# A written order for TensorE and VectorE in the first stage of a three-stage kernel, from its second tile on

## The chip, the cores and the metric

The kernel runs on one core of a Trainium2 chip. The metric is the device time of one execution in microseconds (us). A core has TensorE (PE, matmuls and transposes), VectorE (DVE), ScalarE (ACT), GpSimd (POOL) and SyncE (SP, which issues the transfers here). Each has an instruction queue of its own and waits on semaphores for the others. Matmuls write PSUM, eight banks; everything else lives in SBUF or in DRAM.

## What is computed

Three computations follow one another. Attention runs in chunks of 64 tokens, for 8 heads of 64; its output, 4608 tokens by 512, goes through an RMS norm and a gated layer of width 1536, and the result through a second layer of width 2048:

```python
attn = softmax(scale * q @ k.T) @ v                  # per chunk of 64 tokens and head
x = attn / rms(attn) * rms_g                         # [4608, 512]
x = (silu(x @ w_gate) * (x @ w_val)) @ moe_w_out     # 512 -> 1536 -> 512
h = x @ w_in                                         # 512 -> 2048
out = (h * cos(h)) @ moe2_w_out                      # 2048 -> 512
```

The weights arrive as 64-bit words and are converted on the chip to pairs of 32-bit numbers (a high and a low part). Every product of two such pairs is three matmuls (high by high, high by low, low by high).

## The kernel before, in words

The kernel is one Python function that traces instructions; a scheduler then puts them in an order for each engine and adds the semaphores. The scheduler works with a model of the engines and may move an instruction ahead of one that was written earlier, as long as no dependency forbids it. Tiles come from pools: a tag with `bufs=n` has n buffers, and who takes a buffer again waits until its last readers are done.

The first stage does attention, the norm and the gated product. It goes over 9 tiles of 512 tokens. The first tile is done in halves of 256 tokens, while the gate and value weights are still being converted. The changed loop covers the other eight tiles, `i` from 1 to 8.

In a tile, `gated(f, ...)` runs for 12 blocks of columns `f`: 12 matmuls into a PSUM tile `g`, then 12 into `v`; ScalarE computes `sg` = Silu of `g`, and VectorE multiplies it with `v` into `h`, which is stored to DRAM (`hd`) in pairs of `f`. `g` and `v` have three PSUM buffers each. The operand is `xt`, the normed attention output of the tile, as a high and a low part.

Between these groups stand other pieces of work, placed by `Slots`: a counter that goes up after the `g` and again at the end of every `gated`, so 24 slots in a tile. `slots.after(k, fn)` runs `fn` in k slots from now. Two kinds of work are placed so:

- Attention for the next tile, two pairs of 128-token units in a tile. A pair has six steps (`ATT`). `att_s`: scores `sc` on TensorE, then on VectorE the row maximum `mx` and the difference `p`. `att_e`: Exp on ScalarE. `att_n`: VectorE divides by the row sum `z`. `att_t`: TensorE transposes `p` into `pt`, ScalarE copies it to `pts`. `att_v`: TensorE makes `o`; ScalarE squares it and sums (the instruction writes `xn` and `ss`), GpSimd makes the factor `rs`, VectorE the normed `xn`. `att_x`: TensorE transposes `xn` into `tr`; ScalarE casts it to the high part of `xt`, VectorE subtracts for the low part. `sc`, `pt`, `o` and `tr` share two PSUM buffers.
- Weight conversions for the later stages, 44 in all (`w_tick`). One takes a raw block that was loaded earlier (two buffers), turns it into `wt` (Abs on ScalarE, L102, then four instructions on VectorE, L103 to L106), splits it with a cast on ScalarE and a subtraction on VectorE (L109, L110), and stores `wout` to DRAM (`kout` or `kin`). Of the 44, 28 are of a long kind (for the two output weights), which makes four sums `wsum` besides (L185) and has two casts and two subtractions; 16 are of a short kind. `wt`, `wsum` and `wout` have one buffer each: the casts of a conversion wait until the store of the one before has landed.

Stages two (`b<-xo,w` with 384 columns), three (`h<-xt,w`) and four (`b<-w,xo`) follow and are not touched.

Of the kernel before, what the change touches and what calls it, by code (L numbers as in the profile page):

```python
# [25 lines left out]
N1 = F1 // P  # L26
# [6 lines left out]
TILE = 512  # L33
# [14 lines left out]

HI_MIN = 2.0**-15
HI_MAX = (1.875 - 2.0**-14) * 2.0**16  # L50

AHEAD = 5

# [15 lines left out]
def kernel(  # L69
# [25 lines left out]
    def f32(a):  # L95
        return a.bitcast(F32)


    def convert(raw, t):
        w = raw.bitcast(U32).rearrange("p (n t) -> p n t", t=2)  # L100
        lo, hi = w[:, :, 0], w[:, :, 1]
        nc.scalar.activation(f32(t), f32(hi), AF.Abs)  # L102
        nc.vector.tensor_scalar(f32(t), f32(t), HI_MIN, HI_MAX, op0=ALU.max, op1=ALU.min)  # L103
        nc.vector.tensor_scalar(t, t, 3, 0x3FFFFFF8, op0=ALU.logical_shift_left, op1=ALU.bitwise_and)
        nc.vector.scalar_tensor_tensor(t, hi, 0xC0000000, t, op0=ALU.bitwise_and, op1=ALU.bitwise_or)
        nc.vector.scalar_tensor_tensor(t, lo, 29, t, op0=ALU.logical_shift_right, op1=ALU.bitwise_or)  # L106

    def split(to, a, eng):
        nc.scalar.copy(to[:, 0], a)  # L109
        eng.tensor_tensor(to[:, 1], a, f32(to[:, 0]), op=ALU.subtract)  # L110
# [12 lines left out]
    def free(*tags):  # L123
        for tag in tags:
            if not wanted:
                return
            key = kind, i, k = wanted.pop(0)
            place_of[key] = tag
            if kind in ("h", "x2", "g"):
                early[key] = wp.tile([P, 2, H if kind == "h" else D], F32, tag=tag, name="a")  # L130
                rows = slice(0, 2) if kind == "h" else slice(2 * k, 2 * k + 2)
                a = {"h": hd[0][:, k], "x2": x2d[0], "g": gd[0][:, 0]}[kind]
                nc.sync.dma_start(out=early[key], in_=a[:, rows, : early[key].shape[-1]])
                continue
            shape = [P, 2, D] if kind == "in" else [P, 2, 2, 2, P]
            weight[key] = wp.tile(shape, F32R, tag=tag, name="w")
            nc.sync.dma_start(out=f32(weight[key]), in_=kept[kind, i] if kind == "in" else kept[kind, i][:, k])
# [6 lines left out]
    raws = []  # L144
    flip = [0]

    def w_load():
        if todo_w and len(raws) < 2:
            kind, i, half = todo_w.pop(0)
            flip[0] ^= 1  # L150
            raw = wp.tile([P, 4, P], U64, tag=f"p{24 + flip[0]}", name="wraw")
            if kind == "in":
                nc.sync.dma_start(out=raw, in_=w2[i, 0].rearrange("p (a b) -> p a b", b=P))
            else:

                a, m = (w1, 2) if kind == "out1" else (w2, 1)
                c = 4 * (i // 2) + i % 2
                for n, (row, b) in enumerate(((c, 0), (c + 2, 0), (c + 2, 1), (c, 1))):
                    o = b * 2 * P + half * P
                    nc.sync.dma_start(out=raw[:, n, :], in_=a[row, m][:, o : o + P])  # L160
            raws.append((kind, i, half, raw))

    def w_tick():
        if not raws:
            return
        kind, i, half, raw = raws.pop(0)
        t = pp.tile([P, 4, P], U32, tag="pt", name="wt")
        convert(raw.rearrange("p a b -> p (a b)"), t.rearrange("p a b -> p (a b)"))
        t = f32(t)
        if kind == "in":  # L170
            to = pp.tile([P, 2, D], F32R, tag="pout", name="wout")
            split(to, t.rearrange("p a b -> p (a b)"), nc.vector)
            kept[kind, i] = dr.tile([P, 2, D], F32, name=f"kin{i}")
            nc.sync.dma_start(out=kept[kind, i], in_=f32(to))
        else:
            s = pp.tile([P, 4, P], F32, tag="ps", name="wsum")

            if kind == "out1":
                ops = ((t[:, 3, :], t[:, 2, :], ALU.add), (s[:, 0, :], t[:, 0, :], ALU.subtract))
                ops += ((t[:, 0, :], t[:, 3, :], ALU.subtract), (t[:, 1, :], s[:, 1, :], ALU.subtract))  # L180
            else:
                ops = ((t[:, 3, :], t[:, 0, :], ALU.subtract), (t[:, 2, :], s[:, 0, :], ALU.subtract))
                ops += ((t[:, 2, :], t[:, 3, :], ALU.subtract), (t[:, 1, :], s[:, 1, :], ALU.subtract))
            for n, (a, b, op) in enumerate(ops):
                nc.vector.tensor_tensor(s[:, n, :], a, b, op=op)  # L185
            to = pp.tile([P, 2, 7, P], F32R, tag="pout", name="wout")
            split(to[:, :, 0:3, :], t[:, :3, :], nc.vector)
            split(to[:, :, 3:7, :], s, nc.vector)
            g, e = i // 2, i % 2
            if (kind, g) not in kept:  # L190
                kept[kind, g] = dr.tile([P, 7, 2, 2, 2, P], F32, name=f"k{kind}{g}")
            for h in range(2):
                nc.sync.dma_start(out=kept[kind, g][:, :, e, h, half], in_=f32(to[:, h]))
        w_load()
# [49 lines left out]
    def mm3(acc, steps, first):  # L244

        n = len(steps)
        for k, (ah, al, bh, bl) in enumerate(steps):
            for q, (a, b) in enumerate(((ah, bh), (ah, bl), (al, bh))):
                nc.tensor.matmul(  # L249
                    acc, a, b, start=first and k == 0 and q == 0, stop=k == n - 1 and q == 2, skip_group_check=True  # L250
                )
# [21 lines left out]
    with ExitStack() as st:  # L273
# [117 lines left out]
        xts = {}  # L391
# [16 lines left out]
        ATT = (att_s, att_e, att_n, att_t, att_v, att_x)  # L408
        slots = Slots()
# [19 lines left out]
        def gated(f, x, t0, n):  # L429

            acc = []
            for m in range(2):
                z = ps_g.tile([P, D], F32, tag="gv"[m], name="gv"[m])[:, :n]
                ww = w[f, m]
                c = [slice(d * P, (d + 1) * P) for d in range(ND)]
                mm3(z, [(ww[:, 0, c[d]], ww[:, 1, c[d]], x[:, 0, d], x[:, 1, d]) for d in range(ND)], True)
                acc.append(z)
                if m == 0:
                    slots.end()
            sg = tp.tile([P, D], F32, tag="sg", name="sg", bufs=2)[:, :n]  # L440
            nc.scalar.activation(sg, acc[0], AF.Silu)  # L441
            if f % 2 == 0:
                pend[t0] = tp.tile([P, 2, D], F32, tag="h", name="h")[:, :, :n]
            h = pend[t0]
            nc.vector.tensor_tensor(h[:, f % 2], sg, acc[1], op=ALU.mult)  # L445
            if f % 2:
                c = t0 % PIECE
                nc.sync.dma_start(out=hd[t0 // PIECE][:, f // 4, f % 4 - 1 : f % 4 + 1, c : c + n], in_=h)
            slots.end()
# [27 lines left out]
        for k in range(N1 + BEHIND):  # L477
            need1(min(k + 1, N1 - 1))
            for b in range(2):
                f = k - BEHIND * b  # L480
                if 0 <= f < N1:
                    gated(f, xts[0][:, :, :, b * half : (b + 1) * half], b * half, half)
        ntile = NT // TILE
        for i in range(1, ntile):
            if i + 1 < ntile:
                for u in (4 * i + 4, 4 * i + 6):
                    for n, f in enumerate(ATT):
                        slots.after(1 + 11 * ((u % 4) // 2) + 2 * n - n // 3, lambda f=f, u=u: f(u))
            for n in range(6):
                slots.after(2 + 4 * n, w_tick)  # L490
            for f in range(N1):
                gated(f, xts[i], i * TILE, TILE)
                if i == ntile - 1:
                    if f == 0:
                        while raws:
                            w_tick()
                        free("p24", "p25", "p26", "p27")
                    free(f"p{2 * f}", f"p{2 * f + 1}")
        slots.flush()


# [74 lines left out]
    with ExitStack() as st:  # L576
# [3 lines left out]
        raw, xts = {}, {}  # L580
        ntile = NT // TILE
# [56 lines left out]
    with ExitStack() as st:  # L638
# [53 lines left out]
        def add(a, b, tag="o", bufs=3):  # L692
            t = block(tag, bufs)
            nc.vector.tensor_tensor(t, a, b, op=ALU.add)
            return t
# [8 lines left out]
        u = add(z[6], s1, "s6", 1)  # L704
# [79 lines left out]
```

## Time and profile before

| | |
|---|---|
| median of 3 runs | 1796.24 us (1793.16 to 1796.95) |
| the profiled execution | 1800.6 us |
| span in its profile, first to last instruction | 1798.8 us |
| mean granted TensorE clock | 0.985 of full |
| TensorE busy, of the span | 1727.4 us (96%) |
| VectorE busy | 1232.4 us (69%) |
| ScalarE busy | 756.6 us (42%) |

A row of the profile names the line, the engine, the operation, and what it writes and reads; `x12` is a count of instructions that were merged into the row. In brackets stands how long the engine was idle before it, and what ended that. Line numbers are those of the kernel before; in the changed kernel the same lines stand two lower, and from line 484 on three.

### The profile page before, as it was taken

What the parts mean: (1) busy time and instruction counts of PE and PEld (TensorE: products, weight loads), DVE (VectorE), ACT (ScalarE), POOL (GpSimd) and SP (SyncE); (2) the same over time, 40 slices, a digit from 0 to 9 for tenths busy, and PEclk for the clock granted to TensorE, in tenths of its full rate; (3) what the DMA queues carried; (4) which work ended last, traced back from release to release, by engine and by line L of the source; (5) the groups of instructions that cost most, each with busy time, mean ns of one, the idle gap of its engine ahead of it and who ended that gap; (6) DMA issues with size and microseconds to landing.
All of it is one profiled execution on the core that took longest, in us unless ns stands there. A gap on an engine that the chain in (4) does not pass through costs nothing.

```text
span 1798.8 us, 29151 instructions
## 1 busy us (share of the span) xinstructions
PE 1727.4 (96%) x11736; PEld 1539.2 (86%) x11736; DVE 1232.4 (69%) x1825; ACT 756.6 (42%) x1117; POOL 49.3 (3%) x92
## 2 busy tenths in 40 slices
PE   5899899999999999899999999999999899999998
PEld 5897787778888888799999888888888799999998
DVE  6888787787333331477777588888887887777775
ACT  5544455454333321244444344444443444444443
POOL 1210000000000000000000000000000000000000
PEclk8999999999999999999999999999999899999999
DMA  9338877888222216643335743333225823344430
GB/s 368 112 118 265 260 267 255 252 257 255 83 94 82 83 48 221 211 176 141 141 141 204 264 164 123 124 118 123 100 94 186 304 95 118 123 145 142 147 119 30
DMA packets 159799, 294.72 MB, mean 164 GB/s; under 512 B 10288, under 2 KB 96304, under 8 KB 155184
## 3 DMA queue, kind: packets, MB, share of 16 engines
q1 hardware_dynamic: 159664, 292.86, 47.8%
q8 instruction: 92, 1.51, 0.4%
q14 instruction: 43, 0.35, 0.1%
HBM read 173.80 MB, written 119.01 MB: 163 GB/s over the span
## 4 chain that ended last, share of the span: by engine, by line
PE 78%; issue 9%; DVE 5%; DMA 3%; ACT 3%; POOL 2%; SPq 0%; ACTq 0%; DVEq 0%; POOLq 0%
PE b L249 34%; PE h L249 22%; PE v L249 10%; PE g L249 10%; DMA kout<-wout 3%; POOL w L110 1%; PE sc L315 1%; PE pt L354 1%; PE tr L402 1%; DVE wout L110 1%; PE o L368 0%; POOL rs L387 0%; ACT wout L109 0%; DVE h L445 0%; ACT wt L102 0%
## 5 line engine op out<-in xcount | busy, mean ns | idle before, releaser
L249 PE MATMUL h<-xt,w 128*128 128x512 f32 x1728 | 392.3, 389 | 1.3 <-ACT xt L109 1.2
L249 PEld LDWEIGHTS h<-xt,w 128*128 128x128 f32 x1728 | 324.2, 188 | 69.2 <-ACT xt L109 1.5
L249 PE MATMUL b<-w,xo 128*128 128x256 f32 x3024 | 369.9, 285 | 11.7 <-ACT s L723 5.4
L249 PEld LDWEIGHTS b<-w,xo 128*128 128x128 f32 x3024 | 367.3, 194 | 14.5 <-ACT s L723 7.0
L249 PE MATMUL v<-xt,w 128*128 128x512 f32 (+1 forms) x1440 | 327.3, 376 | 2.5 <-POOL w L110 1.6
L249 PE MATMUL g<-xt,w 128*128 128x512 f32 (+1 forms) x1440 | 325.0, 375 | 4.3 <-ACT w L109 2.1
L249 PEld LDWEIGHTS g<-xt,w 128*128 128x128 f32 x1440 | 254.6, 192 | 50.4 <-ACT w L109 2.3
L249 PEld LDWEIGHTS v<-xt,w 128*128 128x128 f32 x1440 | 255.7, 192 | 48.7 <-POOL w L110 2.4
L249 PE MATMUL b<-xo,w 128*128 128x384 f32 x1512 | 266.5, 335 | 12.4 <-ACT s L559 5.7
L249 PEld LDWEIGHTS b<-xo,w 128*128 128x128 f32 x1512 | 261.7, 188 | 17.4 <-ACT s L559 7.6
L241 DVE TENSOR_TENSOR xo<-rawg,xo 128x512 fp32r<-128x512 f32 x210 | 142.6, 688 | 80.1 <-ACT xo L240 78.8
L240 ACT CAST xo<-rawg 128x512 fp32r<-128x512 f32 x210 | 128.3, 620 | 159.3 <-PE b L249 96.3
L445 DVE TENSOR_TENSOR h<-sg,v 128x512 f32<-128x512 f32 (+1 forms) x120 | 75.3, 629 | 173.8 <-PE v L249 172.1
L441 ACT ACTIVATE sg<-g 128x512 f32<-128x512 f32 (+1 forms) x120 | 66.2, 552 | 171.7 <-PE g L249 155.3
L625 ACT ACTIVATE k<-h 128x1024 int32<-128x1024 f32 x72 | 73.5, 1021 | 142.2 <-PE h L249 142.2
L241 DVE TENSOR_TENSOR xo<-rawh,xo 128x768 fp32r<-128x768 f32 x102 | 94.1, 954 | 51.6 <-ACT xo L240 51.6
L612 ACT ACTIVATE r<-r,halfpi 128x1024 f32<-128x1024 f32 x72 | 82.5, 1145 | 91.2 <-DVE r L611 91.2
L240 ACT CAST xo<-rawh 128x768 fp32r<-128x768 f32 x102 | 81.8, 835 | 89.0 <-DMA rawh<-hd 41.4
L609 DVE SCALAR_TENSOR_TENSOR r<-k,h 128x1024 f32<-128x1024 int32 x72 | 87.6, 1217 | 39.9 <-ACT k L625 39.9
L613 DVE TENSOR_TENSOR r<-r,h 128x1024 f32<-128x1024 f32 x72 | 87.6, 1216 | 34.2 <-ACT r L612 34.1
L610 DVE SCALAR_TENSOR_TENSOR r<-k,r 128x1024 f32<-128x1024 int32 x72 | 87.8, 1220 | 0.9
L109 ACT CAST wout<-wt 128x384 fp32r<-128x384 f32 (+1 forms) x44 | 24.3, 552 | 123.4 <-DMA kout<-wout 63.9
(85 smaller groups left out, 1281.0 us busy)
## 6 DMA issues: line engine op xcount, KB each, us to landing
gd<-r SPq DMA_DIRECT2D x72, 512.0 KB, 2.6
rawg<-gd SPq DMA_DIRECT2D x35, 1024.0 KB, 7.3
kout<-wout SPq DMA_DIRECT2D x56, 448.0 KB, 4.4
w<-kout SPq DMA_DIRECT2D x49, 512.0 KB, 4.2
hd<-h SPq DMA_DIRECT2D x48, 512.0 KB, 3.6
rawh<-hd SPq DMA_DIRECT2D x15, 1536.0 KB, 8.7
qk<-in_qk_dram SPq DMA_DIRECT2D x36, 512.0 KB, 5.2
wraw<-in_w_dram SPq DMA_DIRECT2D x112, 128.0 KB, 3.5
```

The costliest lines, as they stand in the source:

```text
L109: nc.scalar.copy(to[:, 0], a)
L110: eng.tensor_tensor(to[:, 1], a, f32(to[:, 0]), op=ALU.subtract)
L240: nc.scalar.copy(o[:, 0], a)
L241: nc.vector.tensor_tensor(o[:, 1], a, f32(o[:, 0]), op=ALU.subtract)
L249: nc.tensor.matmul(acc, a, b, start=first and k == 0 and q == 0, stop=k == n - 1 and q == 2, skip_group_check=True)
L441: nc.scalar.activation(sg, acc[0], AF.Silu)
L445: nc.vector.tensor_tensor(h[:, f % 2], sg, acc[1], op=ALU.mult)
L609: nc.vector.scalar_tensor_tensor(r, k, -PI2_HI, h, op0=ALU.mult, op1=ALU.add)
L610: nc.vector.scalar_tensor_tensor(r, k, -PI2_LO, r, op0=ALU.mult, op1=ALU.add)
L612: nc.scalar.activation(r, r, AF.Sin, bias=halfpi)
L613: nc.vector.tensor_tensor(r, r, h, op=ALU.mult)
L625: nc.scalar.activation(k, h, AF.Copy, scale=INV2PI, bias=0.25)
```

## The change

The loop over the eight tiles is put into `tc.manual_schedule(engines=ORDERED)` with TensorE and VectorE: on these two engines the scheduler keeps the order in which the instructions are written. ScalarE, GpSimd and SyncE are ordered by the scheduler as before. The slots of the attention steps change too: before, a tile's first pair stood at slots 1, 3, 5, 6, 8, 10 and its second at 12, 14, 16, 17, 19, 21; now at 0, 1, 3, 6, 8, 10 and 12, 13, 15, 18, 20, 22. The conversions keep their slots (2, 6, 10, 14, 18, 22), but are no longer moved from there on VectorE.

```diff
+ET = mybir.EngineType
+ORDERED = {ET.PE, ET.DVE}
...
         ntile = NT // TILE
-        for i in range(1, ntile):
-            if i + 1 < ntile:
-                for u in (4 * i + 4, 4 * i + 6):
-                    for n, f in enumerate(ATT):
-                        slots.after(1 + 11 * ((u % 4) // 2) + 2 * n - n // 3, lambda f=f, u=u: f(u))
-            for n in range(6):
-                slots.after(2 + 4 * n, w_tick)
-            for f in range(N1):
-                gated(f, xts[i], i * TILE, TILE)
...
+        with tc.manual_schedule(engines=ORDERED):
+            for i in range(1, ntile):
+                if i + 1 < ntile:
+                    for u in (4 * i + 4, 4 * i + 6):
+                        for n, f in enumerate(ATT):
+                            slots.after(12 * ((u % 4) // 2) + (0, 1, 3, 6, 8, 10)[n], lambda f=f, u=u: f(u))
+                for n in range(6):
+                    slots.after(2 + 4 * n, w_tick)
+                for f in range(N1):
+                    gated(f, xts[i], i * TILE, TILE)
...
```

ScalarE in the tile `i` = 1, from the copies `pts` of its second pair to the Square that writes `xn`; numbers behind the names tell buffers apart. Before:

```order
L356 COPY pts_2247<-pt_2242 128x512
L356 COPY pts_2254<-pt_2249 128x512
L109 CAST wout_2956<-wt_2945 128x384
L109 CAST wout_2956<-wsum_2951 128x512
L102 ACTIVATE wt_3052<-wraw_2832 128x512
L441 ACTIVATE sg_2306<-g_2256 128x512
L109 CAST wout_3063<-wt_3052 128x384
L109 CAST wout_3063<-wsum_3058 128x512
L102 ACTIVATE wt_3201<-wraw_2963 128x512
L383 ACTIVATE xn_2349,ss_2350<-o_2310 128x512
L383 ACTIVATE xn_2357,ss_2358<-o_2311 128x512
L441 ACTIVATE sg_2391<-g_2365 128x512
```

The same pair on ScalarE in the changed kernel:

```order
L358 COPY pts_2262<-pt_2257 128x512
L358 COPY pts_2269<-pt_2264 128x512
L111 CAST wout_2282<-wt_2271 128x384
L111 CAST wout_2282<-wsum_2277 128x512
L104 ACTIVATE wt_2424<-wraw_2182 128x512
L443 ACTIVATE sg_2393<-g_2312 128x512
L385 ACTIVATE xn_2364,ss_2365<-o_2325 128x512
L385 ACTIVATE xn_2372,ss_2373<-o_2326 128x512
L443 ACTIVATE sg_2460<-g_2397 128x512
L407 CAST xt_2018<-tr_2410 128x4x128
L407 CAST xt_2018<-tr_2417 128x4x128
L111 CAST wout_2435<-wt_2424 128x384
```

Between the copies and the Squares stood the casts of two conversions; now those of one stand there, and the next conversion's casts come after `xt`. Up to this place 12 conversions had been started before, and now 6.

VectorE at the same pair, around `xn`. Before:

```order
L445 TENSOR_TENSOR h_2240<-sg_2306,v_2293 128x512
L110 TENSOR_TENSOR wout_3063<-wt_3052,wout_3063 128x384
L110 TENSOR_TENSOR wout_3063<-wsum_3058,wout_3063 128x512
L103 TENSOR_SCALAR wt_3201<-wt_3201 128x512
L104 TENSOR_SCALAR wt_3201<-wt_3201 128x512
L388 SCALAR_TENSOR_TENSOR xn_2349<-o_2310,rs_2354,gamma_64 128x512
L388 SCALAR_TENSOR_TENSOR xn_2357<-o_2311,rs_2362,gamma_64 128x512
L105 SCALAR_TENSOR_TENSOR wt_3201<-wraw_2963,wt_3201 128x512
L106 SCALAR_TENSOR_TENSOR wt_3201<-wraw_2963,wt_3201 128x512
```

The same place on VectorE in the changed kernel:

```order
L112 TENSOR_TENSOR wout_2282<-wsum_2277,wout_2282 128x512
L447 TENSOR_TENSOR h_2242<-sg_2308,v_2295 128x512
L390 SCALAR_TENSOR_TENSOR xn_2364<-o_2325,rs_2369,gamma_64 128x512
L390 SCALAR_TENSOR_TENSOR xn_2372<-o_2326,rs_2377,gamma_64 128x512
L447 TENSOR_TENSOR h_2395<-sg_2393,v_2380 128x512
L408 TENSOR_TENSOR xt_2018<-tr_2410,xt_2018 128x4x128
L408 TENSOR_TENSOR xt_2018<-tr_2417,xt_2018 128x4x128
L105 TENSOR_SCALAR wt_2424<-wt_2424 128x512
L106 TENSOR_SCALAR wt_2424<-wt_2424 128x512
```

The pieces of two conversions that stood around `xn` are gone from there; a conversion is now whole, and the next starts behind `xt`.

## Rows read from the trace of the kernel before

**Rows 1.** The page's head.
```profile
span 1798.8 us, 29151 instructions
```

**Rows 2.** Busy time by stretch: PE, weight loads, DVE, ACT, POOL, clock, DMA share, GB/s.
```profile
131.10:217.80 86.70, 78.57 (x578) 63.84 (x577) 68.78 (x151) 41.67 (x72) 3.65 (x8) 0.94 0.88 261
217.80:296.70 78.90, 76.14 (x577) 62.25 (x576) 59.99 (x110) 38.98 (x64) 3.61 (x8) 0.98 0.77 263
296.70:378.50 81.80, 76.69 (x578) 62.27 (x578) 65.82 (x140) 40.57 (x68) 3.19 (x8) 0.98 0.83 252
...
527.00:601.10 74.10, 74.10 (x577) 61.15 (x576) 25.03 (x44) 23.98 (x38) 2.95 (x8) 1.00 0.25 86
...
209.00:217.00 8.00, 7.76 (x29) 6.42 (x30) 7.54 (x16) 3.37 (x6) 0.31 (x1) 0.70 0.83 246
```

**Rows 3.** Waits of TensorE from 131.1 to 741 us: total, times, longest.
```profile
PE tr L402 <- DVE xn L388: 12.9, 6, 5.2
PE pt L354 <- DVE p L346: 2.9, 1, 2.9
```

**Rows 4.** Timeline around one wait for `xn`: start us, us, instruction.
```profile
197.25 1.16 PE L368 MATMUL o<-v,pts 64*64 64x64 f32 x64
...
198.21 0.51 ACT L109 CAST wout<-wt 128x384 fp32r<-128x384 f32 x1 [4.98 <-DMA kout<-wout]
...
204.99 0.51 ACT L109 CAST wout<-wt 128x384 fp32r<-128x384 f32 x1 [4.49 <-DMA kout<-wout]
...
206.70 0.58 ACT L383 ACTIVATE xn<-o 128x512 f32<-128x512 f32 x1
...
209.24 2.02 PE L402 MATMUL tr<-ident,xn 128*128 128x128 f32 x8 [5.16 <-DVE xn L388]
...
210.91 4.35 PE L249 MATMUL g<-xt,w 128*128 128x512 f32 x12
```

**Rows 5.** Timeline of TensorE in a tile without waits.
```profile
479.63 1.16 PE L368 MATMUL o<-v,pts 64*64 64x64 f32 x64
...
486.31 1.03 PE L402 MATMUL tr<-ident,xn 128*128 128x128 f32 x8
...
489.92 2.88 PE L249 MATMUL g<-xt,w 128*128 128x512 f32 x12
492.73 1.16 PE L315 MATMUL sc<-qk 64*64 64x64 f32 x64
...
507.56 1.03 PE L354 MATMUL pt<-ident,p 128*128 128x128 f32 x8
...
513.98 1.16 PE L368 MATMUL o<-v,pts 64*64 64x64 f32 x64
```

**Rows 6.** Timelines of VectorE and ScalarE: one conversion's ends, then steps of attention.
```profile
160.00 0.43 DVE L103 TENSOR_SCALAR wt<-wt 128x512 f32<-128x512 f32 x1 [1.33 <-ACT wt L102]
...
165.13 0.69 DVE L110 TENSOR_TENSOR wout<-wsum,wout 128x512 fp32r<-128x512 f32 x1 [0.69 <-ACT wout L109]
...
462.16 0.69 DVE L343 TENSOR_REDUCE z<-p 128x8 f32<-128x512 f32 x1
...
463.32 0.69 DVE L346 TENSOR_TENSOR p<-p,z 128x512 f32<-128x512 f32 x1
...
483.43 0.75 DVE L388 SCALAR_TENSOR_TENSOR xn<-o,rs,gamma 128x512 f32<-128x512 f32 x1 [0.15 <-POOL rs L387]
...
487.62 1.29 DVE L406 TENSOR_TENSOR xt<-tr,xt 128x512 fp32r<-128x512 f32 x2 [2.84 <-ACT xt L405]
...
495.13 1.28 DVE L331 TENSOR_TENSOR p<-sc,mx 128x512 f32<-128x512 f32 x2
...
508.20 1.07 ACT L356 COPY pts<-pt 128x512 f32<-128x512 f32 x2 [2.56 <-PE pt L354]
```

**Rows 7.** The stores `kout`, 56 of them: time to landing; and ScalarE's waits, 145 to 435 us.
```profile
DMA to landing us min/median/max: 3.3/4.3/7.8
ACT wout L109 <- DMA kout<-wout: 54.8, 16, 5.0
```

More of the change, by code (lines that the diff above doesn't have):

```diff
@@ L483 @@
         ntile = NT // TILE
-        for i in range(1, ntile):
-            if i + 1 < ntile:
-                for u in (4 * i + 4, 4 * i + 6):
-                    for n, f in enumerate(ATT):
-                        slots.after(1 + 11 * ((u % 4) // 2) + 2 * n - n // 3, lambda f=f, u=u: f(u))
-            for n in range(6):
-                slots.after(2 + 4 * n, w_tick)
-            for f in range(N1):
-                gated(f, xts[i], i * TILE, TILE)
[L493 to L498, printed above, removed]
+        with tc.manual_schedule(engines=ORDERED):
[8 more added lines that the diff above has]
+                    gated(f, xts[i], i * TILE, TILE)
+                    if i == ntile - 1:
+                        if f == 0:
+                            while raws:
+                                w_tick()
+                            free("p24", "p25", "p26", "p27")
+                        free(f"p{2 * f}", f"p{2 * f + 1}")
         slots.flush()
```

## The prediction, as it was put on record

> **What bounds the kernel now.** I read the page first, then a table of engine busy time by stretch, then the waits, and only then single instructions. The span is 1798.8 us [rows 1]; the execution around it took 1800.6 us, 4.4 us over the median of the three runs shown. I work on the profiled execution and take the difference over to the median unscaled, 1796.24.
>
> Cut the first stage at the starts of its 512-token tiles [rows 2]. A tile in the middle of the stage (527.0 to 601.1) takes 74.1 us with TensorE busy throughout at full clock, and VectorE busy for only 25.0 us of it. The tiles that start at 131.1, 217.8 and 296.7 have the same number of matmuls but take 86.7, 78.9 and 81.8 us. In them VectorE is busy 60 to 69 us, and the granted clock is below 1. The reader should see that the same TensorE work is 12.6, 4.8 and 7.7 us longer while the weight conversions are under way: 25.1 us together. The fourth tile is only 0.3 us over and I leave it out.
>
> The waits of TensorE over these eight tiles are two lines [rows 3]: the transposes `tr` wait for `xn` six times, 12.9 us, and `pt` waits once for `p`, 2.9 us. That is 15.8 us. The other 9.3 us is clock: after the 5.16 us wait at 209.2 a group of twelve matmuls took 4.35 us [rows 4], and the mean granted clock from 209 to 217 is 0.70 [rows 2], part of the stretch at 1.2 instead of 2.4 GHz.
>
> Why was `xn` late? Follow one case [rows 4]. `o` leaves TensorE from 197.25 on, 1.2 us long. ScalarE's Square of it starts at 206.70, 8 us after `o` was there. Between them, in ScalarE's queue, stand the casts of two weight conversions, which waited 4.98 and 4.49 us for the previous conversion's store (kout) because `wout` has one buffer. So the stall is a queue effect: the scheduler put conversions closer together than one store allows, and attention's Square behind them. All 44 conversions lie between about 120 and 438 us, 7.2 us apart; one needs 5.2 us of VectorE [rows 6] and then a store that lands in 4.3 us at the median [rows 7]. ScalarE stood 54.8 us behind such stores [rows 7].
>
> **Busy time against tile lengths.** By the busy row the lost time in the three tiles is 8.1 + 2.8 + 5.1 = 16.0 us [rows 2]. The Trainium skill (Perfetto Trace Analysis, Identifying the Most-Contended Engine) says that busy time of matmuls is a poor measure and the busy share of weight loads a good one. By weight loads, 61.15 of 74.1 us is what a clean tile shows, and 63.84, 62.25 and 62.27 us would fill 77.4, 75.5 and 75.5 us: 9.3 + 3.4 + 6.3 = 19.0 us lost, a sum of 1777. The trace agrees that busy time hides loss, but weight loads grow too at the low clock; the tile lengths decide, and my sum goes by them alone.
>
> **The change, part by part.** No instruction is added or removed. Per tile there are 24 groups of matmuls and two attention pairs before and after, so a tile without waits costs 74.1 us again.
>
> *Conversions at fixed places.* Six per tile, that is one per four slots or 12.4 us on average, in place of 7.2 us. In ScalarE's new order the Square stands ahead of the next conversion's casts. This removes the cause above, if the written order brings no new wait. I check that on one half tile with conversions of the long kind, from clean rows [rows 5]: from `sc` to `pt` 14.8 us with five groups between; the changed order has six in every half, and the sixth is what is left of a half tile, 37.05 - 14.83 - 6.42 - 6.68 - 6.42 = 2.7 us. So with `sc` at 0: `pt` at 17.5, `o` at 24.0, `tr` at 30.6, next `sc` at 37.05.
>
> VectorE in written order [rows 6]: `p` is done 3.7 us after `sc` starts (496.41 less 492.73); `h` 0.7 (4.4); conversion 5.2 (9.6; 160.00 to 165.82 less an `h` of 0.6 in it); `h` (10.3); two normalisations of 1.85 us each (14.0). `pt` needs this at 17.5. From the previous half comes a debt: `tr` at 30.6, `xt` done 2.6 later (33.2), conversion (38.4), `h` (39.1), while `sc`'s result is there at 38.2: 0.9 us late. So the slack at `pt` is 2.6 us. The copies after `pt` end 1.7 us after it starts, `o` follows 6.4 us after: slack 4.7. Then `h` and the second conversion, whose casts stand behind the copies: VectorE is free by about 23. `xn` is done 4.55 us after `o` starts, `tr` comes 6.7 after [rows 5, 6]: slack 2.1. At the tile boundary the second `tr` is now one group later in the tile: only `v` stands between it and the next tile's first `g`, 3.6 us after `tr` starts, and `xt` is ready after 2.6: slack 1.0, the smallest. VectorE's load in a half tile is 15.6 (three conversions) + 4.2 + 2.5 + 3.7 + 1.7 + 1.3 = 29.0 of 37.05 us. For the 16 conversions of the short kind all of this is easier. So the new waits are priced at nothing; what hides them are the slacks just named.
>
> *The stores.* From the end of a conversion to the casts of the next it is 6.3 us at the closest place (38.4 to 37.05 + 4.4 + 0.9 + 2.4 = 44.7). A store lands in 3.3 to 7.8 us, 4.3 at the median [rows 7], and the queue will be less crowded than at 0.77 to 0.88 DMA share [rows 2]. At the longest landing the casts are 1.5 to 2 us late, inside the 2.6 of `pt`.
>
> *What is late next.* The last two conversions now run in the last tile, after its first `h`: some 10 us of VectorE plus one wait for a store, up to about 20 us into the tile. The second `h` waits for them; TensorE wants its PSUM buffer back with the fifth `v`, 24.5 us into the tile. Their raw buffers, which take out1 weights next, come free later too, but these loads belong to the next stage. TensorE's clean tiles show no dearer matmul when VectorE is busy, so I add nothing there.
>
> **Sum.** 12.6 + 4.8 + 7.7 = 25.1 us saved, 0 added. Profiled: 1800.6 - 25.1 = 1775.5. Median: 1796.24 - 25.1 = **1771.1 us**. Bounds: 25.4 us is all that the stage has to give (fourth tile included); less the runs' spread downwards (1796.24 to 1793.16, 3.1 us) and as much again, since one execution's waits stand here for all, that is 1765 at the low end.
>
> **Rivals.**
> 1. *The tile boundary eats part.* If `xt` is 1.5 to 2.5 us later than in the clean row (ScalarE or VectorE still busy), the 1.0 of slack is gone and each of seven boundaries waits 0.5 to 1.5 us: 3.5 to 10.5 us back; with the low clock after some of them (9.3 per 15.8 us of waits), up to 17. Time 1775 to 1788, middle 1781. For it: the place is tighter than before by a group. Against: in the new ScalarE order the casts of `xt` stand ahead of the conversion's.
> 2. *The written order turns store waits into TensorE stalls: slower.* VectorE's conversion waits in the middle for ScalarE's cast, and the cast for a store; behind it now stand `h` and the normalisation that `pt` needs. The Trainium skill (PSUM — Partial Sum Buffer, Engine vs sequencer instructions) states that VectorE's and ScalarE's queues are strictly first in, first out, which speaks against fixing the order. The rows of before show such blocking [rows 4]. It costs from a landing of 6.3 + 2.6 = 8.9 us on; 28 long conversions are 9.3 half tiles, so 25.1 us is eaten at 2.7 us each, a landing of 11.6 us every time; at 13 us it would be 4.1 x 9.3 = 38 us of waits, 1809. Against: the longest landing in the trace is 7.8.
> 3. *No change.* The stall was in ScalarE's queue, which the change does not order; only if ScalarE's program had kept the Square behind casts would nothing be won (1796). The order listed says otherwise. VectorE as a bound would need conversions of 7.9 us (37.05 - 29.0 over three, added to 5.2), every time.
>
> **Chances.** Forecast (22 to 28 us saved) 0.78; rival 1, 0.12; rival 3 and the landing near 11 us, 0.04; rival 2 beyond it, 0.06. A difference of 0.2% (3.6 us) is about what a measurement of this kernel can tell from none. Faster 0.90, same 0.04, slower 0.06. The range for 8 in 10: from 1765 to 1784, the lower part of rival 1 included. The forecast alone: 1765 to 1775.
>
> **What would show it.** All tiles but the last at 74.1 us and granted clock 1.00; no line of `tr` or `pt` waits; ScalarE's wait for kout mostly gone; conversions spread to about 690 us; VectorE's busy share nearly even from 131 to 675. Wrong would be: waits of `g` for `xt` at tile starts (rival 1), or of `pt` for `p` beside long waits of the casts for kout (rival 2).

## The result, and the profile after

| | before | after |
|---|---|---|
| median | 1796.95 us (1793.16 to 1800.97, 5 runs) | 1773.65 us (1772.46 to 1775.03, 5 runs) |
| ratio to before, 95% interval | | 0.9866, [0.9855, 0.9876] |
| profiled execution | 1800.6 us | 1775.03 us |

The medians are 23.3 us apart, the two profiled executions 25.6 us (1800.6 - 1775.03); 25.1 was forecast. The head of the page of after:

```profile
span 1773.2 us, 29106 instructions
```

Cut at the starts of its tiles, as in [rows 2] (columns: length, busy time and count of PE, weight loads, DVE, ACT, POOL, then clock, DMA share, GB/s):

```profile
131.40:205.50 74.10, 74.10 (x578) 61.15 (x577) 47.62 (x97) 29.26 (x51) 2.97 (x8) 1.00 0.59 187
205.50:279.70 74.20, 74.20 (x578) 61.20 (x578) 51.19 (x105) 30.88 (x54) 2.97 (x8) 1.00 0.65 203
279.70:353.80 74.10, 74.10 (x577) 61.15 (x576) 43.82 (x80) 28.76 (x49) 2.97 (x8) 1.00 0.53 183
...
576.20:650.40 74.20, 74.20 (x578) 61.22 (x577) 51.20 (x105) 30.87 (x54) 2.97 (x8) 1.00 0.58 181
```

The tiles that lasted 86.7, 78.9 and 81.8 us are like all others now: TensorE busy throughout, at full clock. VectorE's work did not shrink, it is spread: 43 to 51 us in each of seven tiles, where three had 60 to 69, the fourth 56 and the later ones 25. The waits of TensorE from 110 to 741 us, the answer to [rows 3]:

```profile
PE b L251 <- ACT xo L242: 3.9, 5, 2.0
PE b L251 <- DVE xo L243: 1.7, 3, 0.6
PE tr L404 <- DVE xn L390: 1.3, 2, 1.0
```

The `tr` line is in the first tile, which the change does not touch; `b` belongs to the second stage. From 131 to 715 us the view lists nothing. The step that stalled [rows 4] and a tile boundary, in a timeline of after (start, length, instruction):

```profile
195.26 1.16 PE L370 MATMUL o<-v,pts 64*64 64x64 f32 x64
...
196.46 0.60 ACT L385 ACTIVATE xn<-o 128x512 f32<-128x512 f32 x1 [0.49 <-PE o L370]
...
199.00 0.75 DVE L390 SCALAR_TENSOR_TENSOR xn<-o,rs,gamma 128x512 f32<-128x512 f32 x1 [0.16 <-POOL rs L389]
...
201.93 1.03 PE L404 MATMUL tr<-ident,xn 128*128 128x128 f32 x8
...
203.24 1.29 DVE L408 TENSOR_TENSOR xt<-tr,xt 128x512 fp32r<-128x512 f32 x2 [2.90 <-ACT xt L407]
...
205.54 2.88 PE L251 MATMUL g<-xt,w 128*128 128x512 f32 x12
```

The Square starts 1.2 us after `o` does (9.5 in [rows 4]), `xn` is done at 199.75, 2.2 us before `tr`, and `xt` at 204.53, 1.0 us before the next tile's first `g`. Stores and ScalarE's waits, the answer to [rows 7]; first the group of `kout`, then the page's lines of its two parts (KB each, median us to landing):

```profile
DMA to landing us min/median/max: 3.4/4.5/10.8
...
kout<-wout SPq DMA_DIRECT2D x56, 448.0 KB, 4.3
w<-kout SPq DMA_DIRECT2D x49, 512.0 KB, 4.7
```

The group holds the 56 stores and also 49 loads that read them back (`w<-kout`), and so it does in the rows of before. The 10.8 us is one of four loads issued from 675.6 to 677.8 us, behind the last store. The trace tells the landing of 42 of the 56 stores: 6.2 us at the longest, where before a store took 7.8. The page's median for the stores alone is 4.3 us, and 4.4 before.

Then ScalarE's waits from 145 to 435 us:

```profile
...
ACT wout L111 <- issue: 12.6, 4, 3.2
ACT wout L111 <- DVE wt L108: 12.4, 4, 3.1
ACT wt L104 <- DVE wout L112: 9.1, 12, 0.8
```

The 54.8 us behind `kout` are gone. Where the view says `issue`, the cast starts just as VectorE's last instruction on `wt` ends (206.85 us, and 206.09 + 0.69), so these casts too waited for VectorE and not for a store. In the whole first stage one cast waited for a store, 2.9 us, in the last tile.

### The profile page after: what moved, and what is told of

Read it like the earlier page. It is cut to its first block, busy times and chain, and to the rows that moved or that the text cites. A ratio compares the mean times of both kernels' runs of the same rounds, so it can differ in the third digit from the quotient of the medians.

```text
span 1773.2 us, 29106 instructions
## 1 busy us (share of the span) xinstructions
PE 1718.3 (97%) x11736; PEld 1534.8 (87%) x11736; DVE 1243.9 (70%) x1825; ACT 738.4 (42%) x1103; POOL 46.9 (3%) x92
## 4 chain that ended last, share of the span: by engine, by line
PE 92%; DVE 3%; issue 2%; ACT 1%; POOL 1%; DMA 1%; DVEq 0%; POOLq 0%; ACTq 0%
PE b L251 35%; PE h L251 22%; PE v L251 16%; PE g L251 15%; PE sc L317 1%; PE o L370 1%; PE tr L404 1%; PE pt L356 1%; POOL w L112 1%; DMA x2d<-x 0%; DVE t L107 0%; ACT s L562 0%; ACT s L726 0%; DMA rawh<-hd 0%; DVE t L108 0%
## 5 line engine op out<-in xcount | busy, mean ns | idle before, releaser
L251 PE MATMUL g<-xt,w 128*128 128x512 f32 (+1 forms) x1440 | 318.3, 370 | 4.3 <-ACT w L111 2.1
L443 ACT ACTIVATE sg<-g 128x512 f32<-128x512 f32 (+1 forms) x120 | 66.4, 553 | 288.6 <-PE g L251 287.1
L390 DVE SCALAR_TENSOR_TENSOR xn<-o,rs,gamma 128x512 f32<-128x512 f32 x36 | 27.0, 751 | 78.1 <-POOL rs L389 78.1
```

The lines of the kernel that those rows point to most:

```text
L251: nc.tensor.matmul(acc, a, b, start=first and k == 0 and q == 0, stop=k == n - 1 and q == 2, skip_group_check=True)
L390: nc.vector.scalar_tensor_tensor(xn, o, rs, gamma, op0=ALU.mult, op1=ALU.mult)
```

## The experiments

Twelve runs. Their times are medians; before was 1796.6 to 1798.4 us beside them. Differences under some 3 us are not read: the first tile, which lies ahead of the change, ended up to 3.5 us apart between profiled executions (the next tile's `sc`, in the same slot, starts at 130.74, 131.61 and 134.22 us in the VectorE-only run, the ScalarE-only run and after). Where less counts, the distance from one tile's `sc` to the next one's does.

### Which engine's order matters

Three kernels with one engine held to the written order, and one with the new slots but no written order.

```diff
-ORDERED = {ET.PE, ET.DVE}
+ORDERED = {ET.DVE}
```

> Only VectorE is held to the written order, TensorE's instructions are placed by the scheduler again (they come out in the same order). Theory (the gain is that ScalarE's casts no longer stand ahead of the Square, through conversions 12.4 us apart): conversions stay every three groups, so 1771 to 1776 us and no wait of tr or pt in tiles 2 to 8. Rival (the gain is TensorE's written order): back to 1790 us or more.

```diff
-ORDERED = {ET.PE, ET.DVE}
+ORDERED = {ET.PE}
```

> Only TensorE is held to the written order, VectorE's conversions are placed by the scheduler and come packed again. Theory (packed conversions and their stores cause the stall): 1790 to 1800 us, waits of tr for xn of 10 us and more in all, ScalarE again some 50 us behind kout. Rival (TensorE's written order and the new attention slots are what helps): 1771 to 1780 us.

```diff
-ORDERED = {ET.PE, ET.DVE}
+ORDERED = {ET.Activation}
```

> The kernel after with ScalarE alone held to the written order; the scheduler places VectorE's and TensorE's instructions. TensorE's order comes out the same, VectorE's conversions come apart from each other again and are interleaved with attention's normalisation. Theory (ScalarE's queue decides, the casts behind the Square and 12.4 us apart): 1771 to 1777 us, no tr waits. Rival (it takes VectorE's written order): 1785 us or more.

The kernel before with the slots of after:

```diff
-                        slots.after(1 + 11 * ((u % 4) // 2) + 2 * n - n // 3, lambda f=f, u=u: f(u))
+                        slots.after(12 * ((u % 4) // 2) + (0, 1, 3, 6, 8, 10)[n], lambda f=f, u=u: f(u))
```

> The kernel before with the new attention slots alone, no written order. Theory: the conversions are packed as before, so 1788 to 1800 us with tr waits as before. Rival (the new slots, with pt six groups after sc, give the gain): 1771 to 1780 us.

| in written order | median, us | ratio to before |
|---|---|---|
| VectorE | 1772.54 | 0.9863 [0.9849, 0.9876] |
| ScalarE | 1772.42 | 0.9863 [0.9849, 0.9876] |
| TensorE | 1807.04 | 1.0051 [1.0038, 1.0063] |
| none, new slots | 1803.69 | 1.0036 [1.0023, 1.0048] |

VectorE alone or ScalarE alone gives all of the gain, without a TensorE wait from 131 to 715 us; TensorE's order gives none. A conversion runs on both engines in turn, so pinning it on one holds it back on the other: the last `kout` store is issued at 666.0 and 664.9 us there (669.4 in after), and at 438.2 with TensorE alone. There the conversions are packed again, and ScalarE's waits from 145 to 435 us are those of before, only longer (54.8 there):

```profile
ACT wout L111 <- DMA kout<-wout: 77.9, 20, 6.1
```

TensorE's waits in the same run, 131 to 715 us:

```profile
PE tr L404 <- DVE xn L390: 14.4, 9, 4.1
PE o L370 <- ACT pts L358: 2.3, 2, 2.2
...
```

Both packed kernels came out slower than the range given for them: the new slots without the order are worse than the old ones, by 6.3 us (1803.69 to 1797.41). In the run with the new slots alone `tr` waits for `xn` as before (12.7 us), and waits that before did not have come on top: `g` for `xt` 3.6 us and `o` for `pts` 2.2.

### Store or queue: the packed order with two buffers

The kernel before, `wout` in two buffers, both lines of `w_tick`:

```diff
-to = pp.tile([P, 2, 7, P], F32R, tag="pout", name="wout")
+to = pp.tile([P, 2, 7, P], F32R, tag="po2", name="wout", bufs=2)
```

> The kernel before with two wout buffers in place of one and nothing else; the conversions stay packed. Theory (the casts' wait for the previous conversion's store is what holds ScalarE's queue): ScalarE's 54.8 us behind kout fall below 10 us, most of TensorE's 15.8 us of waits go, 1774 to 1784 us. Rival (the packing itself, VectorE at 60 to 69 us in a tile, makes xn late, whatever the store does): the waits stay above 10 us, 1788 to 1797 us.

1786.94 us, ratio 0.9947 [0.9934, 0.9961]: outside both ranges, and my theory as put there falls short. The waits for the store are gone as it said; ScalarE's, 145 to 435 us:

```profile
ACT wout L109 <- DVE wt L106: 80.1, 36, 4.0
...
ACT wout L109 <- DMA kout<-wout: 3.4, 1, 3.4
```

But ScalarE stands as long at the same casts, now for VectorE's part of the conversion, and TensorE still waits from 131 to 715 us:

```profile
PE tr L402 <- DVE xn L388: 8.1, 11, 2.0
PE pt L354 <- DVE p L346: 1.8, 2, 1.6
```

One of them in the timeline of this run:

```profile
270.03 1.16 PE L368 MATMUL o<-v,pts 64*64 64x64 f32 x64
...
271.28 0.66 ACT L102 ACTIVATE wt<-wraw 128x512 f32<-128x512 f32 x1 [0.26 <-DVE wout L110]
...
274.35 0.63 ACT L109 CAST wout<-wt 128x512 fp32r<-128x512 f32 x1 [2.41 <-DVE wt L106]
...
275.74 0.66 ACT L102 ACTIVATE wt<-wraw 128x512 f32<-128x512 f32 x1 [0.76 <-DVE wout L110]
276.30 0.58 ACT L383 ACTIVATE xn<-o 128x512 f32<-128x512 f32 x1
```

`o` ends at 271.19 and its Square starts at 276.30, behind two conversions' instructions that no store holds. So the Square's place in ScalarE's queue costs time by itself. The second buffer also let the conversions come closer still: the last `kout` store is issued at 403.7 us, 438.5 before. What was open: is it the place, or the density (VectorE busy 63 to 69 us in a tile of 78)?

### Order, density, buffers, one at a time

The kernel after with ten conversions per tile, and `wout` in two buffers, in one, and in one with ScalarE alone ordered:

```diff
-                for n in range(6):
-                    slots.after(2 + 4 * n, w_tick)
+                for n in range(10):
+                    slots.after(2 + 12 * n // 5, w_tick)
```

> The kernel after with two wout buffers and ten conversions per tile in place of six (7.4 us apart, about as dense as before), both engines in written order. With two buffers the store is out of the way. Theory A (what is left of the stall with two wout buffers is the Square's place behind the casts, not the density): the written order cures it, 1771 to 1778 us. Theory B (at this density VectorE itself is the bound): five long conversions and the rest make 13.4 + 5 x 5.2 = 39.4 us of VectorE in a half tile of 37.05, so tiles 2 to 4 last 3 to 6 us longer and TensorE waits for p, xn or xt: 1783 to 1797 us.

> The kernel after with ten conversions per tile in place of six and the one wout buffer of before: density and buffer are those of before, the order is written. If the scheduler's order of ScalarE's queue makes before's loss alone: 1771 to 1778 us, as with two buffers. If the written order at this density has a store's wait in it (a conversion's casts come 6.2 to 9.3 us behind the last one's, store and the rest of the conversion take 9.7): ScalarE stands 20 us and more behind kout, VectorE behind ScalarE, and p, xn or xt are late: 1783 to 1800 us.

> The same with ScalarE alone in written order, so that VectorE's h and normalisations may be placed between the parts of a conversion. If it is the store's wait in ScalarE's queue that costs, the time is that of the run with both engines in order, within some 4 us. If VectorE's strict order behind the waiting cast makes the cost, this one is faster by 5 us or more, 1772 to 1779 us.

| conversions | order | `wout` buffers | median, us |
|---|---|---|---|
| packed | the scheduler's (before) | 1 | 1797.4 |
| packed | the scheduler's | 2 | 1786.94 |
| ten per tile | written | 1 | 1784.45 |
| ten per tile | written | 2 | 1776.61 |
| ten per tile | written, ScalarE alone | 1 | 1786.42 |
| six per tile | written (after) | 1 | 1773.65 |

Density by itself is not the bound: theory B falls. With two buffers and the written order TensorE is busy throughout a stretch as long as a tile in which VectorE has more work than in any tile of after (66.4 us to 51.2):

```profile
353.40:427.50 74.10, 74.10 (x576) 60.79 (x574) 66.42 (x144) 37.68 (x66) 2.97 (x8) 1.00 0.92 278
```

The 3 us that this run lies over after are no more than the bound above; `g` waits at three tile starts, 1.8 us in all:

```profile
PE g L251 <- DVE xt L408: 1.8, 3, 0.7
```

With one buffer the store is back; the ScalarE waits of that run, 131 to 700 us:

```profile
ACT wout L111 <- DVE wt L108: 43.0, 19, 6.0
ACT wout L111 <- DMA kout<-wout: 29.5, 10, 5.9
```

and TensorE waits at tile starts, 131 to 715 us:

```profile
PE g L251 <- ACT xt L407: 3.2, 2, 1.6
PE g L251 <- DVE xt L408: 2.3, 3, 0.9
...
```

A buffer more is worth 10.5 us in the scheduler's order (1797.4 - 1786.94) and some 7 to 8 in the written one (1784.45 - 1776.61 is 7.8; before was 1.1 us slower beside the first of the two); the written order at this density is worth 10.3 us with two buffers and some 13 to 14 with one. The new slots are part of what is called the written order here. Which engine is ordered matters little: ScalarE alone, 1786.42, is 2 us off.

### The worked-out slacks

The kernel after with the old slots:

```diff
-slots.after(12 * ((u % 4) // 2) + (0, 1, 3, 6, 8, 10)[n], lambda f=f, u=u: f(u))
+slots.after(1 + 11 * ((u % 4) // 2) + 2 * n - n // 3, lambda f=f, u=u: f(u))
```

> The kernel after with the attention steps at their old slots; the written order stays. Slack theory: in the first half of a tile pt follows sc by five groups (14.8 us), p is ready about 16.5 us after sc, so pt waits some 1.5 to 3 us in each of up to seven tiles, more with low clock after some: 1780 to 1793 us. Rival (the written order alone gives the gain, the slots do nothing): 1771 to 1777 us.

1783.05 us, ratio 0.9921 [0.9908, 0.9935], as the slack theory has it. TensorE's waits, 131 to 715 us:

```profile
PE pt L356 <- DVE p L348: 7.9, 7, 1.1
```

Seven times, once per tile: TensorE has the first unit's `p` in time and stands 1.1 us for the second one's. Both normalisations come behind an `h` that VectorE can start only at 222.27 us, when its `v` is done, and `pt` starts at 224.87. The tile takes 75.66 us (285.55 - 209.89, `sc` to `sc`) in place of 74.14 (282.49 - 208.35). With this order the old slots cost 9.4 us.

The kernel after with the transposes a slot later:

```diff
-slots.after(12 * ((u % 4) // 2) + (0, 1, 3, 6, 8, 10)[n], lambda f=f, u=u: f(u))
+slots.after(12 * ((u % 4) // 2) + (0, 1, 3, 6, 8, 11)[n], lambda f=f, u=u: f(u))
```

> The kernel after with the transposes one slot later (11 and 23 in place of 10 and 22), so that the second one stands right ahead of the next tile's first g. Slack theory: xt is ready 2.6 us after tr starts and only the transposes themselves (0.8 us) lie between, so g waits 1.8 us at each of seven tile starts, 12.6 us, and some low clock behind: 1784 to 1794 us. Rival (the tile boundary has slack that my sum did not see): 1771 to 1777 us.

1784.65 us, ratio 0.9931 [0.9918, 0.9945], as the slack theory has it. One boundary in the timeline:

```profile
202.57 1.03 PE L404 MATMUL tr<-ident,xn 128*128 128x128 f32 x8
...
203.82 1.29 DVE L408 TENSOR_TENSOR xt<-tr,xt 128x512 fp32r<-128x512 f32 x2 [0.28 <-ACT xt L407]
204.33 0.50 PE L251 MATMUL g<-xt,w 128*128 128x512 f32 x1 [0.73 <-ACT xt L407]
205.16 2.76 PE L251 MATMUL g<-xt,w 128*128 128x512 f32 x11 [0.33 <-DVE xt L408]
207.85 1.16 PE L317 MATMUL sc<-qk 64*64 64x64 f32 x64
```

From `tr` to `sc` it is 5.28 us here and 3.70 at the second `sc` of the same tile (165.50 to 169.20), where nothing waits: 1.6 us per boundary, seven times 11.1, and the medians are 11.0 apart. This is rival 1 of the prediction, made by moving one step by one slot.

### Rival 2 on purpose: conversions in pairs

The kernel after with the second of two conversions right behind the first, with one `wout` buffer and with two:

```diff
-                    slots.after(2 + 4 * n, w_tick)
+                    slots.after(2 + 8 * (n // 2), w_tick)
```

> The kernel after with the same conversions in pairs, back to back (slots 2, 2, 10, 10, 18, 18), so that the second one's casts stand behind the first one's store in VectorE's written order. Rival 2 of the prediction, made on purpose: VectorE stands behind a store of 4 us, p is ready near 20 us after sc instead of 17.5, and pt or tr wait 2 to 5 us in most tiles with long conversions: 1785 to 1810 us. Rival (the written order has room for a store's wait too): 1771 to 1778 us.

> The kernel after with the conversions in pairs and with two wout buffers, so that a pair has no store between its halves. If the store's wait makes half of the pairs' loss and the two conversions' own 10 us of VectorE ahead of the normalisation the other half: ScalarE's wait for kout goes from 41 us to under 5, p is ready some 1.5 us after pt wants it instead of 3, 1781 to 1789 us. If the store alone is at fault: 1772 to 1778 us. If the store has no part: 1796 to 1800 us.

One buffer: 1798.06 us, ratio 1.0006 [0.9998, 1.0015], the whole gain lost. Two: 1781.7 us, 0.9916 [0.9903, 0.993]. A stall of the first run in its timeline:

```profile
226.18 0.52 ACT L111 CAST wout<-wt 128x384 fp32r<-128x384 f32 x1 [3.13 <-DMA kout<-wout]
...
226.72 0.56 DVE L112 TENSOR_TENSOR wout<-wt,wout 128x384 fp32r<-128x384 f32 x1 [2.65 <-ACT wout L111]
...
229.61 0.69 DVE L348 TENSOR_TENSOR p<-p,z 128x512 f32<-128x512 f32 x1
...
230.44 0.63 PE L356 MATMUL pt<-ident,p 128*128 128x128 f32 x4 [2.59 <-DVE p L348]
```

The cast waits for the store, VectorE for the cast, and the normalisation that `pt` needs stands behind. The rule on strictly first-in, first-out queues (the Trainium skill, PSUM — Partial Sum Buffer, Engine vs sequencer instructions) agrees with this trace. TensorE's waits for `p` in this run, 131 to 715 us:

```profile
PE pt L356 <- DVE p L348: 14.3, 11, 2.6
```

and with two buffers, where ScalarE stands behind `kout` for 2.4 us in place of 41.3:

```profile
PE pt L356 <- DVE p L348: 6.4, 7, 1.1
```

So of the pairs' 24.4 us (1798.06 - 1773.65), 16.4 go with the store and 8.0 stay, two thirds and one third where half and half was expected. What stays stands behind the two conversions: in the run with two buffers they hold VectorE from 211.73 to 222.23 us, the normalisations come after them, and the second half of `pt`, at 226.51, has waited 1.14 us for `p`.

## Why the prediction was right

**Which cause.** Right, with its two halves weighed by the runs: conversions closer than a store allows, and the Square behind their casts. Either half alone makes a loss: with no store in the way the scheduler's order still cost 13.3 us over after (1786.94 - 1773.65), and with the written order a store in the way cost some 7 to 8. The text leaned on the store ("the casts of two weight conversions, which waited 4.98 and 4.49 us for the previous conversion's store"), and taking the store out of the way gave back 10.5 us, less than half of what the change did. The two parts do not simply add: without the store the conversions also stood closer together.

**25.1 us from the tile lengths, 0 added.** Right tile by tile: the seven tiles with attention last from 131.1 to 675.2 us before and from 131.4 to 650.4 after, 25.1 less, and after every one lasts 74.1 or 74.2 us at clock 1.00. The step from one execution to the median was less exact: the medians are 23.3 apart, since the profiled execution of before lay 3.65 us over its median and that of after 1.4 over its own; 1773.65 is 2.6 over the forecast 1771.1. The sum by weight loads, 19.0 us (the Trainium skill, Perfetto Trace Analysis, Identifying the Most-Contended Engine), gave 1777, which is 3.4 over the measured median, so the medians hardly tell the two apart. The tile lengths do: 6.1 us more came back in the tiles than weight loads showed.

**"The other 9.3 us is clock"** was a mis-sized term, outside the sum. With two buffers and the scheduler's order the four tiles from 131.1 to 441.6 us are 14.1 us over clean ones and their waits 9.9 us, at a granted clock of 1.00 in all four:

```profile
131.10:210.20 79.10, 75.26 (x578) 61.00 (x577) 67.75 (x151) 42.15 (x72) 3.80 (x8) 1.00 0.99 301
210.20:288.50 78.30, 75.02 (x578) 60.94 (x577) 62.90 (x114) 39.89 (x66) 3.74 (x8) 1.00 0.78 267
288.50:366.00 77.50, 74.98 (x578) 60.96 (x577) 68.68 (x154) 41.15 (x71) 3.80 (x8) 1.00 0.92 279
366.00:441.60 75.60, 74.86 (x578) 61.15 (x577) 45.48 (x96) 31.84 (x53) 3.09 (x8) 1.00 0.65 205
```

So 4.2 us over 13 waits, 0.3 each, are lost beside the listed idle time at that clock; by an estimate at the same rate, seven waits are 2.3 of the 9.3, and some 7 are left for the clock.

**The slacks.** `tr` 2.2 us against 2.1, the tile boundary 1.0 as worked out, and the moved transposes confirmed it to 0.2 us per tile (1.8 expected, 1.6 measured). `pt` has more than the 2.6 given: in the tile whose `sc` starts at 208.35, `p` is done at 222.16 and `pt` starts at 225.91, 3.75; the conversion there took 4.8 us of VectorE, from 213.16 to 217.93, not 5.2, and the `p` ahead of it was done 4.1 us after `sc`, where 3.7 and a debt of 0.9 were counted.

**The stores.** Right. A less crowded queue was expected, and the DMA share is 0.49 to 0.65 in the seven tiles, where the three long ones had 0.77 to 0.88. The longest landing that the trace tells, 6.2 us, is below the 6.3 that was counted between one conversion and the next one's casts, and far below the 8.9 at which rival 2 was to begin; no cast but one waited for a store. The two conversions in the last tile ended as forecast (the last store is issued at 669.4, 19 us into the tile), behind the one wait of 2.9 us, and TensorE did not wait. "Spread to about 690 us", in the list of signs, does not fit with that and was 20 us too late.

**The rivals.** None came true, and two were real: one slot costs 11.0 us (rival 1), conversions back to back 24.4 (rival 2). Rival 3 is what TensorE's order alone gives, or worse.

**A faster kernel** than after is not among these: VectorE or ScalarE alone are 1 us ahead, inside the differences that the first tile makes.

## What to carry to other kernels

When an engine waits for a short step, look at what stands ahead of that step in its own engine's queue, and what that is waiting for; removing the outer wait (here a second buffer) may only put the next one in its place, while the step placed ahead of the side work gave all of the gain here only with room for the store as well: at the old density and with one buffer 10.8 us were still lost (1784.45 - 1773.65). Before an order is fixed by hand, work out the slack at every hand-over from clean rows of the trace, down to the smallest: those here held to 0.2 us at the tile boundary, and said which slot could not be moved. Spread side work that ends in a transfer at least as far apart as its own time and the transfer together.

## What the runs showed that was not expected

A wait costs TensorE more than the idle time that the views list: in the run with late transposes 1.6 us per boundary against 0.73 + 0.33 listed, since the matmuls around it no longer overlap (the `tr` that lasts 1.03 us is followed after 0.8 us where nothing waits). The clock fell after waits that come close together as well: in the run with ten conversions and one buffer `g` waited 1.62 and then 0.94 us, and the eleven matmuls behind took 4.38 us, where eleven in the late-transposes run, behind 0.73 and 0.33, took 2.76:

```profile
205.59 0.50 PE L251 MATMUL g<-xt,w 128*128 128x512 f32 x1 [1.62 <-ACT xt L407]
207.03 4.38 PE L251 MATMUL g<-xt,w 128*128 128x512 f32 x11 [0.94 <-DVE xt L408]
```

The granted clock from 205 to 210 us in that run is 0.71, part of it at 1.2 in place of 2.4 GHz.
